# A fused attention and MLP kernel: a constant table moved to a hardware DMA queue, the last output tile in two column parts, and the planner's due dates moved by seeded steps

## The chip, the cores and the metric

The kernel runs on one core of one Trainium2 chip. The metric is the device time of one execution in microseconds (us), taken as the median of several runs. Runs of one kernel agree within about 0.3%. A comparison is called "faster" or "slower" only beyond 2%, but the 95% intervals of five rounds are about 0.2 to 0.4% wide to each side, so effects of 1 us in 320 us can be seen, though only just.

Engines are abbreviated as in the profile: PE is TensorE (matmuls), PEld its weight loads, DVE is VectorE, ACT is ScalarE, POOL is GpSimd and SP is SyncE. A "q" behind a name (SPq, ACTq) is the sequencer that issues DMAs. DMAs issued by SP and ACT go through hardware queues; those issued by POOL go through a software queue (in the first 14 us of the kernel before the profile lists 704 and 288 packets on two hardware queues and 1146 on one software queue).

## The reference

Four batches of eight heads of block-sparse attention (768 tokens, head size 64, blocks of 32; neighbours, first and last block, and three sampled blocks per block row), followed by an MLP-mixer layer:

```python
scores = scale * q @ k.T                       # masked to -1e9 outside the block pattern
attn   = softmax(scores);  x = attn @ v        # [4, 768, 512] after the heads are joined
a1  = alpha1 * x + beta1
tok = einsum('ts,bsd->btd', w_tok, a1)         # 768 x 768 over tokens
u   = x + lam * tok
a2  = alpha2 * u + beta2
out = u + lam * (relu(a2 @ w_ch1) @ w_ch2)     # 512 -> 2048 -> 512
```

## The kernel before

Heads are worked in 16 pairs. A pair has nine score units of 128 keys x 1024 queries; each unit is one exp on ACT (144 in all, numbered from 0 here). For the first six pairs the mask is a bias that is part of the score matmul: 24 more rows under the 64 rows of q and k. The rows under k are block indicators (`ind`), those under q are made at the start from a constant table (`tab`) and the sampled block numbers (`sampi`). This is the start of the kernel, where all else waits:

```python
    nc.gpsimd.dma_start(tab[MB, :], tab_dr.ap())                        # 4.5 KB, POOL's queue
    nc.sync.dma_start(sampi[MB, :], sampled_blocks.bitcast(I32))
    nc.scalar.dma_start(k2f[:, 0, :], pair_ap(k, 0, 0)[:, 0, :])        # 192 KB: k, first head
    nc.sync.dma_start(q2f[:, 0, :], pair_ap(q, 0, 0)[:, 0, :])
    nc.scalar.dma_start(identb[:], ident_dr.ap())                       # 32 KB: for PE transposes
    nc.sync.dma_start(kx2[0][MB, 0, :], ind_dr.ap())                    # indicator rows
    nc.sync.dma_start(q2f[:, 1, :], pair_ap(q, 0, 0)[:, 1, :])          # second head
    nc.sync.dma_start(k2f[:, 1, :], pair_ap(k, 0, 0)[:, 1, :])
    ...                                                                 # three more indicator copies
    nc.gpsimd.dma_start(ld["v"][0][:], pair_ap(v, 0, 0))
    keep_warm(8, 512)                  # eight matmuls of 512 columns on zeros
    ...                                # DVE: eqt, three maxima, mbb: the bias from tab and sampi
    ...                                # PE: two bias matmuls, mbb x indicator rows
    for w, cp in enumerate((nc.vector.tensor_copy, nc.scalar.copy)):
        t = transposes(gbT[w][:], lambda o: relp[:, 0, w, ts(o, P)], range(3))   # q, then k, head 0
        ...
    keep_warm(5, P)
    for j in range(1, 4):              # bias rows for the second head, and for the other buffer
        nc.sync.dma_start(qx2[j // 2][MB, j % 2, :], qx2[0][MB, 0, :])
```

Everything after this is put in order when the kernel is built. Each operation has an engine, an assumed duration, the operations that it depends on and a due date (a number on a scale of exps). A list scheduler goes through time and gives each free engine, of the operations that are ready, the one with the earliest due date. The order that comes out is fixed in the program; on the chip each engine takes its instructions strictly in that order.

```python
    op = pl.pe(("qk", i), occ, i - 0.7, e_qk, deps=..., ...)          # scores of unit i
    ex = pl.act(("exp", j), act(UN), j, ...)                          # exp of unit j
    pv = pl.pes(("pv", j, a), ..., j + 1.5, ...)                      # attn @ v
    tk = pl.pes(("tok", pi, g, j), NT, pe(1, P), FINE if pi < 4 else NT,
                dd + 1 + g, ...)                                      # token matmuls of pair pi
```

The channel MLP (`ch1`, `ch2`) ends the kernel; the last output tile is 16 matmuls of 512 columns, one add on DVE and one store of 256 KB.

The softmax here doesn't subtract the row's maximum and nothing guards it: scores larger than these inputs give would overflow.

## Time and profile before

| | before |
|---|---|
| time | 319.65 us, median of 4 (319.15 to 320.06) |
| span of the profiled run | 318.3 us |
| PE, DVE, ACT busy | 96%, 72%, 57% |
| first score matmul / exp 0 / exp 10 start | 8.22 / 9.27 / 20.58 us |
| last add to the end | 314.54 to 318.27: 3.73 us |

The chain of work that ended last, by engine, from the page of the kernel before:

```profile
PE 87%; ACT 6%; issue 3%; DVE 1%; DMA 1%; ACTq 0%; POOLq 0%
```

PE is the bottleneck, so only time that PE loses can be won. Busy time does not show this loss well, because the ends of matmuls are modelled. I took the start-to-start time of neighbouring matmuls instead, with the median of each form as its cost (32 ns for 65 columns, 56 for 128, 162 for 384, 216 for 512), and filled in records that are missing from the trace. What is left over is called PE loss below. It is 4.4 us up to 8.2 us (of which 1.4 us are the warm-up matmuls at half speed), 2.9 us from 8.2 to 14.4, 0.3 from there to 20, 3.3 us from 20 to 60, and then about 1 us in each 20 us until 240, which comes from a change of form: a score matmul on 64 rows costs about 95 ns more when it follows another form and when another follows it. After 260 us there is none. So the places to look at are the first 60 us and the tail.

The start, from the timelines of DVE and PE of the kernel before (start us, duration us, engine, line, operation, output<-input, shapes, count, idle time before it and what ended it):

```profile
5.39 0.22 DVE L358 TENSOR_TENSOR eqt<-sampi,tab 24x72 f32<-24x72 int32 x1 [4.16 <-DMA tab<-tab_c]
6.28 0.17 DVE L367 TENSOR_SCALAR mbb<-tab 24x24 bf16<-24x24 f32 x1
6.50 0.33 PE L388 MATMUL sps<-qk,mbb 24*24 24x384 bf16 x1 [1.96 <-DVE mbb L367]
6.92 0.51 PE L383 MATMUL gb<-identb,relp 128*128 128x128 bf16 x6
8.22 1.01 PE L821 MATMUL sps<-qk 88*128 88x512 bf16 x3 [0.51 <-DVE qk L402]
```

DVE stands 4.16 us for the table, then makes the bias; PE stands 1.96 us for the bias, transposes q and k with the identity matrix and starts the first scores at 8.22 us.

Busy time by stretch, from the windows of the kernel before (start:end, length, then busy us and count of each engine, the granted clock of PE, the time of the DMA packets as a share of the 16 DMA engines' time, which can come out over 1, GB/s):

```profile
core 0: us, PE busy (x) PEld busy (x) DVE busy (x) ACT busy (x) POOL busy (x), PEclk, DMA share, GB/s
8.20:14.40 6.20, 6.18 (x41) 4.03 (x41) 2.39 (x6) 4.28 (x5) 5.08 (x9) 0.50 1.08 155
20.00:60.00 40.00, 38.41 (x641) 31.44 (x639) 34.08 (x73) 35.93 (x41) 19.31 (x29) 1.00 1.20 214
```

In the first stretch PE runs at half speed: 41 matmuls fill 6.2 us. The clock record has the half speed from 7.57 to 14.40 us, that is 6.83 us or two times 3.41. The Trainium skill, "TensorE: Matmul & The Clock Gate", section "Part 1: The HAM clock gate", describes a free-running activity window of 3413 ns after which the clock is set; this trace agrees with that length. The second line is the stretch in which exps on ACT and the work of PE take turns: ACT is busy 35.93 of 40 us.

In that stretch, ACT's waits of the kernel before, from 20 to 62 us (engine line <- who ended the wait: us in total, times, longest):

```profile
ACT eT L850 <- PE sps L821: 3.9, 4, 1.9
```

And one place of it, from the timeline of PE of the kernel before:

```profile
30.63 0.59 PE L821 MATMUL sps<-qk 88*128 88x512 bf16 x3
31.45 2.17 PE L1088 MATMUL gb<-a1p,wtokT 128*128 128x128 bf16 x36 [0.23 <-ACT qk L428]
33.46 1.03 PE L821 MATMUL sps<-qk 88*128 88x512 bf16 x5
```

Token matmuls come as one block of 36. While it runs, PE makes no scores for ACT; in other places PE has only scores and waits for ACT to free their banks.

The tail of the kernel before, from the timeline at 314 to 318 us:

```profile
314.54 0.69 DVE L1295 TENSOR_TENSOR ot<-x_sb,gb 128x512 f32<-128x512 f32 x1 [2.77 <-PE gb L1273]
315.25 0.33 SPq L1314 DMA_DIRECT2D out_dram<-ot  x1
```

### The profile page before, as it was taken

Reading aid. Unit: us, or ns where it says so; the run is one execution under the profiler, and the core shown is the slowest. Engines: PE = TensorE matmul, PEld = TensorE weight load, DVE = VectorE, ACT = ScalarE, POOL = GpSimd, SP = SyncE. Lnnn points to the kernel's source line nnn. Section 1 sums busy time; section 2 is a strip of 40 time slices with the busy share of each in tenths; the row PEclk is TensorE's granted clock in tenths of the full one; section 3 lists DMA queues with packets and bytes.
Section 4 is the critical chain, followed back from the end, with each engine's and each line's share of the span. In section 5 each row is a group of like instructions: output and inputs, shape, how many; then the busy total and the mean of one; then the engine's idle time right before and its main releaser. Section 6 shows DMA issues by size and latency. Waiting matters only on the chain.

```text
span 318.3 us, 7655 instructions
## 1 busy us (share of the span) xinstructions
PE 306.7 (96%) x3204; PEld 188.5 (59%) x3237; DVE 230.5 (72%) x431; ACT 180.9 (57%) x217; POOL 55.9 (18%) x88
## 2 busy tenths in 40 slices
PE   5999999999999999999999999999999999999995
PEld 2677877756565665465656565655656565555542
DVE  3468979965879887697878696978778776555531
ACT  3799998788877557667685666666575400000000
POOL 3747354212404040213010100101000000000000
PEclk9599999999999999999999999999999999999999
DMA  6999999998737366276441411232102001100011
GB/s 147 152 243 208 209 203 205 202 134 138 116 59 140 69 115 129 60 136 127 58 113 55 101 59 53 69 96 61 27 33 60 33 2 47 55 33 33 35 66 66
DMA packets 46594, 31.40 MB, mean 99 GB/s; under 512 B 27192, under 2 KB 42016, under 8 KB 46560
## 3 DMA queue, kind: packets, MB, share of 16 engines
q0 software_dynamic: 16976, 17.44, 33.7%
q1 hardware_dynamic: 29296, 13.24, 15.8%
q8 instruction: 25, 0.41, 0.5%
q10 hardware_dynamic: 288, 0.23, 0.3%
q14 instruction: 9, 0.07, 0.1%
HBM read 30.86 MB, written 6.29 MB: 117 GB/s over the span
## 4 chain that ended last, share of the span: by engine, by line
PE 87%; ACT 6%; issue 3%; DVE 1%; DMA 1%; ACTq 0%; POOLq 0%
PE gb L1215 26%; PE gb L1273 25%; PE gb L876 11%; PE gb L1088 10%; PE sps L840 8%; ACT eT L850 5%; PE sps L821 5%; DMA tab<-tab_c 1%; PE gb L383 1%; PE sps L626 1%; ACT qk L428 1%; DVE x_sb L1112 0%; ACT uT L428 0%; DVE ub L1119 0%; PE gb L581 0%
## 5 line engine op out<-in xcount | busy, mean ns | idle before, releaser
L850 ACT ACTIVATE eT<-sps 128x1024 f16<-128x1024 f32 x144 | 140.5, 1025 | 37.6 <-PE sps L840 29.2
L1215 PE MATMUL gb<-uT,w1b 128*128 128x384 bf16 x512 | 100.8, 326 | 0.0
L1273 PE MATMUL gb<-w2b,hts 128*128 128x512 bf16 x351 | 91.4, 379 | 1.9 <-issue 0.3
L857 DVE TENSOR_TENSOR eT<-eT,msk 128x1024 f16<-128x1024 f16 x90 | 60.4, 684 | 10.1 <-ACT eT L850 10.1
L1245 DVE TENSOR_SCALAR hts<-gb,b1t 128x384 bf16<-128x384 f32 x75 | 46.2, 616 | 27.4 <-PE gb L1215 26.9
L1215 PEld LDWEIGHTS <-w1b 128*128 128x128 bf16 x512 | 46.4, 98 | 32.9 <-issue 1.2
L876 PEld LDWEIGHTS <-eT 128*128 128x128 f16 x1152 | 49.7, 98 | 24.7 <-issue 5.9
L876 PE MATMUL gb<-vext,eT 128*128 128x65 f16 x1152 | 57.3, 194 | 0.0
L1273 PEld LDWEIGHTS <-hts 128*128 128x128 bf16 x384 | 35.0, 98 | 32.8 <-issue 1.2
L1237 ACT ACTIVATE hts<-gb,b1t 128x384 bf16<-128x384 f32 x53 | 30.8, 582 | 29.7 <-PE gb L1215 27.8
L1088 PE MATMUL gb<-a1p,wtokT 128*128 128x128 bf16 x576 | 36.7, 219 | 0.2 <-ACT qk L428 0.2
L821 PE MATMUL sps<-qk 88*128 88x512 bf16 (+1 forms) x144 | 33.8, 342 | 2.0 <-ACT eT L850 1.2
L1088 PEld LDWEIGHTS <-wtokT 128*128 128x128 bf16 x576 | 33.5, 98 | 3.9 <-issue 1.5
L777 POOL DMA_DIRECT2D qk<-qk x20 | 12.2, 616 | 127.3 <-DMA qk<-q 71.3
L840 PE MATMUL sps<-qk 64*128 64x512 bf16 (+1 forms) x240 | 27.3, 326 | 0.1
L1295 DVE TENSOR_TENSOR ot<-x_sb,gb 128x512 f32<-128x512 f32 x24 | 16.5, 686 | 11.2 <-PE gb L1273 10.6
L1112 DVE TENSOR_TENSOR x_sb<-x_sb,gb 128x384 f32<-128x384 f32 x32 | 17.6, 551 | 9.5 <-PE gb L1088 9.4
L895 DVE TENSOR_TENSOR x_sb<-gb,rcp 128x384 f32<-128x384 f32 x32 | 17.8, 557 | 1.1
L1119 DVE TENSOR_TENSOR ub<-x_sb,a_bc 128x384 bf16<-128x384 f32 x32 | 17.7, 553 | 0.6
L821 PEld LDWEIGHTS <-qk 88*128 88x128 bf16 x144 | 13.0, 101 | 7.5 <-issue 2.7
L840 PEld LDWEIGHTS <-qk 64*128 64x128 bf16 x240 | 8.0, 94 | 15.0 <-issue 12.1
L1053 DVE TENSOR_TENSOR a1p<-a1p,b_bc 128x768 bf16<-128x768 bf16 (+1 forms) x20 | 15.8, 792 | 0.3
(66 smaller groups left out, 150.3 us busy)
## 6 DMA issues: line engine op xcount, KB each, us to landing
out_dram<-ot SPq DMA_DIRECT2D x24, 256.0 KB, 2.0
v<-in_v_dram POOLq DMA_DIRECT2D x16, 192.0 KB, 7.1
q<-in_q_dram POOLq DMA_DIRECT2D x15, 192.0 KB, 7.6
k<-in_k_dram POOLq DMA_DIRECT2D x15, 192.0 KB, 6.8
w1b<-in_moe_w_ch_dram POOLq DMA_DIRECT2D x4, 512.0 KB, 10.6
w2b<-in_moe_w_ch_dram POOLq DMA_DIRECT2D x4, 512.0 KB, 12.5
qk<-qk POOLq DMA_DIRECT2D x20, 96.0 KB, 2.2
wtk<-in_moe_w_tok_dram POOLq DMA_DIRECT2D x3, 384.0 KB, 9.6
```

The lines of the kernel that those rows point to most:

```text
L821: nc.tensor.matmul(spsT[sl(key)][:, o : o + w], kx2[i][0:KC, a, ts(jt, P)], qx2[i][0:KC, a, c : c + w], start=True, stop=True,)
L840: nc.tensor.matmul(spsT[sl(key)][:, o : o + w], kd[i][rows, h, g, :], qx2[i][rows, h, c : c + w], start=True, stop=True,)
L850: nc.scalar.activation(eTt[sl(("eT", i))][:], spsT[sl(key)][:], AF.Exp, bias=EXPB, scale=SCALE)
L857: nc.vector.tensor_tensor(out=e, in0=e, in1=msk[:, :, x : x + 512], op=ALU.mult)
L876: nc.tensor.matmul(bk[:, t * VW : t * VW + D + 1], eTt[sl(("eT", i))][:, ts(col, P)], vx[:, a, jt, 0 : D + 1], start=(r == 0), stop=(r >= ...
L895: nc.vector.tensor_tensor(out=x_sb[:, s0 : s0 + NT, h * D : (h + 1) * D], in0=o[:, :, 0:D], in1=rc[:].unsqueeze(2).broadcast_to([P, NT, D] ...
L1088: nc.tensor.matmul(tp[:, j, :], wtokT[:, s, ts(m * g + j, P)], a1p[sl(ak)][:, s, :], start=(s == 0), stop=(s == NT - 1),)
L1119: nc.vector.tensor_tensor(out=ub[sl(uk)][:, m * g : m * g + m, :], in0=x_sb[:, s0 + m * g : s0 + m * g + m, cs], in1=bc(a2_bc, m), op=ALU. ...
L1215: nc.tensor.matmul(bank(bk)[:, 0:HS], w1b[:, dk, ts(f, P)], uT[b % 3][:, dk, ts(hf, HS)], start=(dk == 0), stop=(dk == 3),)
L1237: nc.scalar.activation(htsT[hk][:, f, :], bank(bk)[:, 0:HS], AF.Relu, bias=b1t[:, f : f + 1], scale=1.0,)
L1245: nc.vector.tensor_scalar(out=htsT[hk][:, f, :], in0=bank(bk)[:, 0:HS], scalar1=b1t[:, f : f + 1], scalar2=0.0, op0=ALU.add, op1=ALU.max,)
L1273: nc.tensor.matmul(bank(ck)[:, 0:DM], htsT[hk][:, nk, ts(mt, P)], w2h["t"][:, nk, :], start=(nk == 0), stop=(nk == 15),)
```

## The change

Its intent: let the bias be ready sooner, shorten the tail, and find a better order. The 21 seeds each move the due dates of a random part of the operations by a random amount; where they come from is not told, but the numbers look like the kept steps of a long random search. The planner's loop is also rewritten to run faster at build time. Shortened:

```diff
+SEEDS = [4000001, 4000004, 4000014, ...]                  # 21 numbers
@@ Op
-        self.due = due
+        self.due = self.due0 = due
@@ Plan.run: candidates and their ready times are kept, not searched for anew (cut)
-                if best:
-                    op, (e, occ, vis) = min(best.values(), key=lambda x: x[0].due)
+                if best:
+                    op, (e, occ, vis) = min(best.values(), key=lambda x: (x[0].due, x[0].n))
@@ start
-    nc.gpsimd.dma_start(tab[MB, :], tab_dr.ap())
     nc.sync.dma_start(sampi[MB, :], sampled_blocks.bitcast(I32))
+    nc.scalar.dma_start(tab[MB, :], tab_dr.ap())
     nc.scalar.dma_start(k2f[:, 0, :], pair_ap(k, 0, 0)[:, 0, :])
-    keep_warm(8, 512)
+    keep_warm(7, 512)
@@ ch2, the output tiles (the slice cs is then used in matmuls, add and store)
-            for mt in range(3):
+            cuts = [(mt, 0, DM) for mt in range(3)]
+            if kk == 2 * B - 1:
+                cuts[2:] = [(2, 0, HS), (2, HS, DM)]         # HS = 384, DM = 512
+            for mt, c0, c1 in cuts:
@@ before pl.run()
+    for seed in SEEDS:
+        r = random.Random(seed)
+        part, step = r.choice([0.01, 0.03, 0.1, 0.3]), r.choice([0.5, 1.5, 4])
+        for op, due in zip(pl.ops, [op.due for op in pl.ops]):
+            if r.random() < part and op.due0 < 80:
+                op.due = due + r.gauss(0, step)
```

The built programs, compared engine by engine, show that table and warm-up alone change nothing else in the order; that the split with the new loop changes, apart from buffer numbers, fewer than a hundred of some 6500 rows on PE (matmuls and weight loads); and that the seeds reorder PE from about its row 85 to about its row 3390, thus in the first half.

More of the change, by code (lines that the diff above doesn't have):

```diff
@@ L1 @@
+import random
 from contextlib import ExitStack
@@ L44 @@
 FINE = 3
+SEEDS = [4000001, 4000004, 4000014, 4000025, 4000032, 4000033, 4000038, 4000259, 4000302, 4000315, 4000516, 4000717, 4000744, 4000751, 4000754, 4000772, 4000823, 4000910, 4001214, 4001220, 4002279]
 ORD = ((0, 2, 4, 1, 3, 5), (1, 3, 5, 0, 2, 4))
@@ L159, in run @@
         t = min(self.free.values())
-        todo = list(self.ops)
+        heirs = {}
+        for n, op in enumerate(self.ops):
+            op.n = n
+            before = {id(d): d for d in op.deps + op.after if d.start is None}
+            op.left = len(before)
+            for d in before:
+                heirs.setdefault(d, []).append(op)
+        cand = [op for op in self.ops if not op.left]
+        for op in cand:
+            op.ready = max([d.vis for d in op.deps] + [0])
+        count = len(self.ops)
         release = []
-        order = []
-        while todo:
+        while count:
             for r in [r for r in release if r[0] <= t]:
@@ L170, in run @@
                 best = {}
-                for op in todo:
-                    if any(d.vis is None or d.vis > t for d in op.deps):
+                idle = [e for e in self.free if self.free[e] <= t]
+                for op in cand:
+                    if op.ready > t:
                         continue
-                    if any(d.start is None for d in op.after):
+                    opts = [o for o in op.opts if o[0] in idle]
+                    r = self.reader.get(op.reads)
+                    if r and r[1] > t:
+                        opts = [o for o in opts if o[0] == r[0]]
+                    opts = [
+                        o
+                        for o in opts
+                        if o[0] not in best
+                        or (op.due, op.n) < (best[o[0]][0].due, best[o[0]][0].n)
+                    ]
+                    if not opts:
                         continue
                     taken = {}
-                    ok = True
                     for need in op.need:
@@ L180, in run @@
                         if p is None:
-                            ok = False
                             break
                         taken[p] = taken.get(p, 0) + 1
-                    if not ok:
-                        continue
-                    r = self.reader.get(op.reads)
-                    for o in op.opts:
-                        e = o[0]
-                        if r and r[0] != e and r[1] > t:
-                            continue
-                        if self.free[e] <= t and (e not in best or op.due < best[e][0].due):
-                            best[e] = (op, o)
-                for op in todo:
-                    if not op.urgent or any(d.vis is None for d in op.deps):
-                        continue
-                    for o in op.opts:
-                        if o[0] in best and best[o[0]][0].due > op.due:
-                            wait = max([d.vis for d in op.deps]) - t
-                            if 0 < wait < best[o[0]][1][1]:
-                                del best[o[0]]
+                    else:
+                        for o in opts:
+                            best[o[0]] = (op, o)
+                if not best:
+                    break
+                for op in cand:
+                    if op.urgent and op.ready > t:
+                        for o in op.opts:
+                            if o[0] in best and best[o[0]][0].due > op.due:
+                                if op.ready - t < best[o[0]][1][1]:
+                                    del best[o[0]]
                 if best:
-                    op, (e, occ, vis) = min(best.values(), key=lambda x: x[0].due)
+                    op, (e, occ, vis) = min(best.values(), key=lambda x: (x[0].due, x[0].n))
                     for need in op.need:
@@ L220, in run @@
                         self.exps += 1
-                    todo.remove(op)
+                    cand.remove(op)
+                    count -= 1
+                    for h in heirs.get(id(op), []):
+                        h.left -= 1
+                        if not h.left:
+                            h.ready = max([d.vis for d in h.deps] + [0])
+                            cand.append(h)
                     op.emit(op)
@@ L225, in run @@
             later += [r[0] for r in release if r[0] > t]
-            later += [d.vis for op in todo for d in op.deps if d.vis is not None and d.vis > t]
-            if todo and not later:
-                raise RuntimeError(f"stuck: {[o.name for o in todo[:20]]}")
-            if todo:
+            later += [op.ready for op in cand if op.ready > t]
+            if count and not later:
+                raise RuntimeError(f"stuck: {[o.name for o in cand[:20]]}")
+            if count:
                 t = min(later)
-        return t
 @with_exitstack
@@ L1265, with e_c2 @@
             pc = []
-            for mt in range(3):
+            cuts = [(mt, 0, DM) for mt in range(3)]
+            if kk == 2 * B - 1:
+                cuts[2:] = [(2, 0, HS), (2, HS, DM)]
+            for mt, c0, c1 in cuts:
                 t = 3 * hf + mt
-                ck = ("cp", kk, mt)
+                cs = slice(c0, c1)
+                ck = ("cp", kk, mt, c0)
                 for r in range(4):
-                    def e_c2(op, hk=hk, ck=ck, mt=mt, r=r):
+                    def e_c2(op, hk=hk, ck=ck, mt=mt, r=r, cs=cs):
                         for nk in range(4 * r, 4 * r + 4):
                             nc.tensor.matmul(
-                                bank(ck)[:, 0:DM],
+                                bank(ck)[:, cs],
                                 htsT[hk][:, nk, ts(mt, P)],
-                                w2h["t"][:, nk, :],
+                                w2h["t"][:, nk, cs],
                                 start=(nk == 0),
@@ L1282 @@
                         ("ch2", kk, mt, r),
-                        pe(4, 2048),
-                        d0 + 18 + (4 * mt + r) * 18 / 12,
+                        pe(4, 4 * (c1 - c0)),
+                        d0 + 18 + (4 * mt + r) * 18 / 12 + c0 / 100,
                         e_c2,
@@ L1291, with e_ot @@
                     pc.append(c2)
-                okey = ("ot", kk, mt)
-                def e_ot(op, okey=okey, ck=ck, b=b, t=t):
+                okey = ("ot", kk, mt, c0)
+                def e_ot(op, okey=okey, ck=ck, b=b, t=t, cs=cs):
                     nc.vector.tensor_tensor(
-                        out=ot[sl(okey)][:],
-                        in0=x_sb[:, b % NXB * NT + t, :],
-                        in1=bank(ck)[:, 0:DM],
+                        out=ot[sl(okey)][:, cs],
+                        in0=x_sb[:, b % NXB * NT + t, cs],
+                        in1=bank(ck)[:, cs],
                         op=ALU.add,
@@ L1303 @@
                     ("ot", kk, mt),
-                    dve(512),
+                    dve(c1 - c0),
                     d0 + 18 + 18 / 12 * 4 * mt - 2,
@@ L1311, with e_out @@
                 OT[(b, t)] = o
-                def e_out(op, okey=okey, b=b, t=t):
+                def e_out(op, okey=okey, b=b, t=t, cs=cs):
                     nc.sync.dma_start(
-                        out[b].rearrange("(p o) d -> p o d", o=NT)[:, t, :], ot[sl(okey)][:]
+                        out[b].rearrange("(p o) d -> p o d", o=NT)[:, t, cs],
+                        ot[sl(okey)][:, cs],
                     )
```

## The prediction

> **What bounds it now.** TensorE (PE): 87% of the chain of waits that ended last. From start-to-start times of the matmuls (median of each form as its cost: 32 ns for 65 columns, 56 for 128, 162 for 384, 216 for 512; absent records filled in) I find hardly a recoverable gap from 60 us on: about 1 us in each 20 us, nearly all of it 95 ns at each entry to and exit from the 64-row score matmuls. What can be won lies before 60 us and after the last matmul:
>
> - Start: `tab` is issued on the GpSimd queue at 1.24 us and lands at 5.37; VectorE waits 4.2 us for it (waits view). The mask bias is ready at 6.45, the bias matmuls start at 6.50 after 2.1 us of idle PE, the first score matmul at 8.22.
> - Clock: half speed from 7.57 to 14.40 us, two windows of 3.41 us; PE loses about 2.9 us. The Trainium skill, "TensorE: Matmul & The Clock Gate", section "Part 1: The HAM clock gate", describes such a window and a throttle after low activity; this trace agrees.
> - 14.4 to 60 us: about 3.6 us of PE loss, mostly before score matmuls that wait for exp on ACT (1.02 us each).
> - Tail: last VectorE add 0.69 us, output DMA 1.98 us, closing 1.0 us: 4.1 us after the last matmul starts.
>
> **What the change does.**
>
> 1. `tab` on the ACT queue. Its neighbours on hardware queues land in 2.0 to 2.5 us. The Trainium skill, "DMA: Bandwidth & Descriptors", section "SWDGE vs HWDGE vs iDMA", also has hardware descriptor generation as the faster setup. So `tab` lands near 2.5 to 2.8 us and the bias is ready near 4.0 (the small VectorE operations took 1.06 us). Seven warm-up matmuls end at 4.18. The bias matmuls start at 4.2 to 4.4 unless the indicator rows (landed only at 5.55 before, behind contention) hold them. The first score matmul is at about 6.1 (5.8 to 7.3): gain 2.0 us.
> 2. With the PE gap nearly closed, the clock may stay full; I give it 60%. It then saves about 2 of the 2.9 us, as ACT becomes the limit. Estimate: 1.2 us.
> 3. Due dates. The order on PE, DVE and ACT changes in the first half: token matmuls and transposes that ran as one block near 31 us are cut up and put between scores. I expect a third of the 3.6 us: 1.2 us; it can be nothing.
> 4. Last tile in 384 and 128 columns: 16 more matmuls, no more PE work (162+56 against 216 ns). The last add is about 0.3 us instead of 0.69, the last transfer 64 KB instead of 256: 0.7 us.
> 5. The rewritten planner loop is build time only: without the seeds the order is nearly the old one.
>
> All of it is on the critical path, as PE runs without gaps afterwards: 2.0 + 1.2 + 1.2 + 0.7 = 5.1 us.
>
> **Prediction: 314.6 us, 312.0 to 317.5.** Faster by over 2% (under 313.4): 0.24; within 2%: 0.74; slower: 0.02.
>
> **What would show it.** Step 1: VectorE idle under 2 us before its first compare, first score matmul near 6.1. Step 2: granted clock over 0.9 in 8 to 20 us (0.73 before). Step 3: less PE idle ended by exp in 14 to 60 us. Step 4: last add to end under 3.1 us (3.73 before).
>
> **What would make it wrong.** The indicator rows still land at 5.5 (1 us less); the clock falls anyway; the new order makes PE stand before operands not yet loaded; or the seeds recover most of the early loss (312).

## The result

| | before | after |
|---|---|---|
| time, median of 4 | 319.65 us (319.15 to 320.06) | 314.70 us (314.35 to 315.75) |
| ratio, 95% interval | | 0.9851 (0.9823 to 0.9880) |
| first score matmul / exp 0 / exp 10 start | 8.22 / 9.27 / 20.58 us | 7.34 / 8.08 / 18.73 us |
| PE loss 8.2 to 14.4 us / 20 to 60 us | 2.9 / 3.3 us | 1.7 / 0.6 us |
| last add to the end | 3.73 us | 2.78 us |

A ratio is the mean time of one kernel's runs over that of the other's of the same rounds, so it is not quite the ratio of the medians. In a later series the same two kernels gave 0.9867 (0.9846 to 0.9887). The change saves 1.3 to 1.5%; by the 2% rule it counts as the same.

The chain that ended last, by engine, from the page of the changed kernel:

```profile
PE 93%; DVE 3%; DMA 1%; issue 1%; ACT 1%; ACTq 0%
```

ACT's share went from 6 to 1%: PE waits for exps hardly at all now. The start, from the timelines of DVE and PE of the changed kernel (line numbers are 19 to 23 higher than before):

```profile
2.50 0.23 DVE L377 TENSOR_TENSOR eqt<-sampi,tab 24x72 f32<-24x72 int32 x1 [1.27 <-DMA sampi<-in_sampled_blocks_dram]
3.39 0.17 DVE L386 TENSOR_SCALAR mbb<-tab 24x24 bf16<-24x24 f32 x1
4.64 0.35 PE L407 MATMUL sps<-qk,mbb 24*24 24x384 bf16 x1 [0.28 <-DMA qk<-ind_c]
6.20 0.49 PE L402 MATMUL gb<-identb,relp 128*128 128x128 bf16 x6 [1.05 <-DMA identb<-ident_c]
7.34 1.33 PE L840 MATMUL sps<-qk 88*128 88x512 bf16 x5 [0.37 <-DVE qk L421]
```

The table no longer holds anything. The bias is ready at 3.56 instead of 6.45 us, 2.9 us sooner, and the bias matmuls start 1.9 us sooner. But a new wait stands behind them: PE waits 1.05 us for the identity matrix, which landed at 4.04 us before and lands at 6.16 us now. The first score matmul is only 0.9 us sooner.

The windows of the changed kernel, the columns as above:

```profile
8.20:14.40 6.20, 6.10 (x67) 4.32 (x65) 3.26 (x8) 5.39 (x6) 3.31 (x6) 0.73 1.13 202
20.00:60.00 40.00, 39.76 (x671) 32.76 (x670) 35.37 (x75) 38.10 (x43) 17.66 (x26) 1.00 1.21 212
```

The clock was at half speed for one window of 3.41 us (8.15 to 11.56 us) instead of two. From 20 to 60 us PE ran 671 matmuls instead of 641, and ACT was busy 38.10 us instead of 35.93. ACT's waits in 20 to 62 us, and the place with the token matmuls in the timeline of PE, both of the changed kernel:

```profile
ACT eT L869 <- PE sps L840: 1.2, 2, 0.8
```

```profile
29.99 1.16 PE L1107 MATMUL gb<-a1p,wtokT 128*128 128x128 bf16 x18
...
31.24 0.60 PE L840 MATMUL sps<-qk 88*128 88x256 bf16 x3
31.67 1.17 PE L1107 MATMUL gb<-a1p,wtokT 128*128 128x128 bf16 x18
32.68 0.60 PE L840 MATMUL sps<-qk 88*128 88x512 bf16 x3
33.12 1.17 PE L1107 MATMUL gb<-a1p,wtokT 128*128 128x128 bf16 x18
```

The block of 36 is cut into parts of 18 with scores between them. The tail, from the timeline of the changed kernel:

```profile
309.03 0.56 DVE L1318 TENSOR_TENSOR ot<-x_sb,gb 128x384 f32<-128x384 f32 x1 [1.91 <-PE gb L1296]
309.61 0.96 SPq L1337 DMA_DIRECT2D out_dram<-ot  x2
309.92 0.29 DVE L1318 TENSOR_TENSOR ot<-x_sb,gb 128x128 f32<-128x128 f32 x1 [0.34 <-PE gb L1296]
```

The last add took 0.29 us instead of 0.69, and from its start to the end it is 2.78 us instead of 3.73.

### The profile page after: what moved, and what is told of

Its sections match the earlier page's. It is cut to its first block, busy times and chain, and to the rows that moved or that the text cites. A ratio compares the mean times of both kernels' runs of the same rounds, so it can differ in the third digit from the quotient of the medians.

```text
span 312.7 us, 7687 instructions
## 1 busy us (share of the span) xinstructions
PE 304.4 (97%) x3221; PEld 188.3 (60%) x3252; DVE 231.4 (74%) x434; ACT 179.7 (57%) x215; POOL 55.7 (18%) x87
## 4 chain that ended last, share of the span: by engine, by line
PE 93%; DVE 3%; DMA 1%; issue 1%; ACT 1%; ACTq 0%
PE gb L1234 27%; PE gb L1296 26%; PE gb L895 12%; PE gb L1107 10%; PE sps L859 8%; PE sps L840 7%; PE gb L402 2%; DMA identb<-ident_c 1%; PE sps L645 1%; DVE qk L449 1%; ACT eT L869 1%; PE gb L600 0%; DVE x_sb L1131 0%; DVE ub L1138 0%; DVE a1p L1072 0%
## 5 line engine op out<-in xcount | busy, mean ns | idle before, releaser
L1296 PE MATMUL gb<-w2b,hts 128*128 128x512 bf16 (+2 forms) x369 | 91.3, 369 | 1.8 <-issue 0.2
L895 PE MATMUL gb<-vext,eT 128*128 128x65 f16 x1152 | 58.0, 194 | 0.1
L1296 PEld LDWEIGHTS <-hts 128*128 128x128 bf16 x400 | 35.7, 97 | 31.2 <-issue 0.7
L1256 ACT ACTIVATE hts<-gb,b1t 128x384 bf16<-128x384 f32 x52 | 30.1, 582 | 28.1 <-PE gb L1234 26.4
L1107 PE MATMUL gb<-a1p,wtokT 128*128 128x128 bf16 x576 | 38.2, 219 | 0.1
L840 PE MATMUL sps<-qk 88*128 88x512 bf16 (+1 forms) x144 | 33.0, 333 | 0.7 <-DVE qk L421 0.4
L1318 DVE TENSOR_TENSOR ot<-x_sb,gb 128x512 f32<-128x512 f32 (+2 forms) x25 | 16.6, 664 | 10.1 <-PE gb L1296 9.6
L1061 DVE TENSOR_TENSOR a1p<-x_sb,a_bc 128x768 bf16<-128x768 f32 (+1 forms) x20 | 15.8, 791 | 0.2
```

The source lines that it names most:

```text
L840: nc.tensor.matmul(spsT[sl(key)][:, o : o + w], kx2[i][0:KC, a, ts(jt, P)], qx2[i][0:KC, a, c : c + w], start=True, stop=True,)
L895: nc.tensor.matmul(bk[:, t * VW : t * VW + D + 1], eTt[sl(("eT", i))][:, ts(col, P)], vx[:, a, jt, 0 : D + 1], start=(r == 0), stop=(r >= ...
L1107: nc.tensor.matmul(tp[:, j, :], wtokT[:, s, ts(m * g + j, P)], a1p[sl(ak)][:, s, :], start=(s == 0), stop=(s == NT - 1),)
L1256: nc.scalar.activation(htsT[hk][:, f, :], bank(bk)[:, 0:HS], AF.Relu, bias=b1t[:, f : f + 1], scale=1.0,)
L1296: nc.tensor.matmul(bank(ck)[:, cs], htsT[hk][:, nk, ts(mt, P)], w2h["t"][:, nk, cs], start=(nk == 0), stop=(nk == 15),)
```

## The experiments

Each run was compared with the kernel before on the same chip in five rounds. All gave correct results. There were four series, not all on the same chip, so ratios are compared, not medians.

### One part at a time

`tab_only` is the kernel before with two edits:

```diff
-    nc.gpsimd.dma_start(tab[MB, :], tab_dr.ap())
+    nc.scalar.dma_start(tab[MB, :], tab_dr.ap())      # behind sampi's issue on sync
-    keep_warm(8, 512)
+    keep_warm(7, 512)
```

> The old kernel with the table on the ACT queue and seven warm-up matmuls; no other change. Theory A (the gain is a sum of independent parts, read from the two traces): the first score matmul comes 0.9 us sooner (near 7.3 instead of 8.2), a throttled window less gives up to 1.2 us; 317.6 to 318.8 us against 319.7. Rival B (what is won at the start is lost again to the exp pace on ACT, so that only the new order brings anything): within 0.3 us of the old kernel. Both expect the identity matrix to land late (near 6 us) and PE to wait for it about 1 us.

`tail_only` is the changed kernel without the seeds, with table and warm-ups as before:

```diff
-    for seed in SEEDS: ...
-    nc.scalar.dma_start(tab[MB, :], tab_dr.ap())
+    nc.gpsimd.dma_start(tab[MB, :], tab_dr.ap())
-    keep_warm(7, 512)
+    keep_warm(8, 512)
```

> The old kernel with the new planner loop and the last tile in parts of 384 and 128 columns; table on GpSimd, eight warm-ups, no seeds. Theory A: last add to end 2.8 us instead of 3.7, so 318.7 us (0.95 less). Rival B: the planner's new loop or the other bank numbers cost something, or the second output transfer queues behind the first, and the gain is under 0.4 us.

`seeds_only` is the changed kernel with the old table, warm-ups and tail:

```diff
-            if kk == 2 * B - 1:
-                cuts[2:] = [(2, 0, HS), (2, HS, DM)]
-    nc.scalar.dma_start(tab[MB, :], tab_dr.ap())
+    nc.gpsimd.dma_start(tab[MB, :], tab_dr.ap())
-    keep_warm(7, 512)
+    keep_warm(8, 512)
```

> The changed kernel with table on GpSimd, eight warm-ups and the last tile whole again: the seeds alone. Theory A (parts add up): PE loss in 20 to 60 us falls from 3.3 to about 0.6 us, 317.0 us (2.7 less). Rival B (the seeded order needs the early start, because it was planned for it): loss in 20 to 60 us stays over 2 us, and the time is over 318.3 us.

`no_seeds` is the changed kernel without the loop over the seeds:

```diff
-    for seed in SEEDS: ...
```

> The changed kernel without the loop over the seeds: table, warm-ups and tail changed, order as planned before. Theory A: 317.4 us (2.7 slower than the changed kernel), PE loss in 20 to 60 us about 3.3 us. Rival B (the early start lets the old order do as well): 315.5 us or less.

Measured:

| kernel | median us | ratio to before (95%) | first score | exp 10 starts | exp 10 to end | PE loss 20 to 60 us |
|---|---|---|---|---|---|---|
| before | 319.8 | 1 | 8.22 | 20.58 | 297.70 | 3.3 |
| tab_only | 318.52 | 0.9968 (0.9949 to 0.9987) | 7.96 | 19.78 | 297.56 | 3.2 |
| tail_only | 318.60 | 0.9967 (0.9944 to 0.9991) | 8.14 | 18.75 | 296.92 | 3.3 |
| seeds_only | 316.68 | 0.9908 (0.9888 to 0.9928) | 8.62 | 20.34 | 294.87 | 0.65 |
| no_seeds | 318.38 | 0.9972 (0.9947 to 0.9997) | 8.25 | 19.57 | 296.77 | 3.3 |
| after (as first measured) | 314.70 | 0.9851 (0.9823 to 0.9880) | 7.34 | 18.73 | 293.97 | 0.59 |

The column "exp 10 to end" is the useful find. It splits a run into a start, which differs from execution to execution, and a rest that repeats to a tenth of a microsecond for kernels of the same order. From it:

- The seeds are worth 297.70 - 294.87 = 2.83 us without, and 296.77 - 293.97 = 2.80 us with the early start and the new tail. So theory A of `seeds_only` holds, and the rival, that the seeded order needs the early start, falls; so does the rival of `no_seeds`, that the early start lets the old order do as well (its PE loss stayed at 3.3 us). The timings agree: 0.9908 is 2.9 us of 319.8.
- The tail is worth 297.70 - 296.92 = 0.78 us, and 294.87 - 293.97 = 0.90 us with the seeds. Between the two kernels without seeds that have the table on ACT's queue (`tab_only` to `no_seeds`) it is 0.79 us. The rival of `tail_only`, a gain under 0.4 us, falls.
- Table and warm-ups act before exp 10 alone, and there they are hard to see. With the table on POOL's queue exp 10 started at 20.58, 18.75 and 20.34 us in the three profiles, with it on ACT's queue at 19.78, 19.57 and 18.73 (and, in later runs, 19.91 and 19.92). The timings say 1.0 us (0.4 to 1.6) for `tab_only`, but `no_seeds` has the tail's 0.8 us too and gains only 0.9 us in all, which leaves about nothing for the table. Between 0 and 1 us is what can be said; neither theory of `tab_only` is excluded.

Both expected a late identity matrix in `tab_only`, and so it was, in the waits of PE of that run:

```profile
PE gb L383 <- DMA identb<-ident_c: 1.3, 1, 1.3
```

The windows of 20 to 60 us of `seeds_only` and of `no_seeds`, in this order, show where the seeds work:

```profile
20.00:60.00 40.00, 39.77 (x673) 32.92 (x671) 35.49 (x75) 38.36 (x43) 19.30 (x28) 1.00 1.19 212
```

```profile
20.00:60.00 40.00, 38.20 (x634) 31.21 (x632) 34.18 (x72) 35.86 (x41) 18.75 (x27) 1.00 1.22 211
```

### What holds the start

The second series had the changed kernel again as its measure.

> The changed kernel once more, as the measure for the next three on the same chip: 314.7 us, 0.985 of the old kernel.

It gave 315.66 us, 0.9867 (0.9846 to 0.9887). Its profiled execution had a worse start than the first one: the identity matrix landed at 7.12 us, the first score matmul came at 8.53 us and exp 10 at 19.91 us, and the rest was 293.97 us again. So one and the same kernel differs by 1.2 us in its start.

`ident_first` issues the identity matrix ahead of k:

```diff
     nc.scalar.dma_start(tab[MB, :], tab_dr.ap())
+    nc.scalar.dma_start(identb[:], ident_dr.ap())
     nc.scalar.dma_start(k2f[:, 0, :], pair_ap(k, 0, 0)[:, 0, :])
-    nc.scalar.dma_start(identb[:], ident_dr.ap())
```

> The changed kernel with the identity matrix issued on the ACT queue before the 192 KB of k, instead of after it. Theory A (PE waits 1.05 us for the identity matrix at 5.1 to 6.2 us, and all later work shifts with it): it lands before 5 us, the first score matmul is near 6.3 instead of 7.3, and the time falls by 0.8 to 1.0 us to 313.8. Rival B (the early part is paced by the exps and by the loads, and slack behind eats an earlier start): the first score matmul is earlier, but the time falls by less than 0.3 us.

Measured: 315.70 us, 0.9874 (0.9857 to 0.9891), no gain against the 0.9867 of the changed kernel. The identity matrix landed at 4.05 us as hoped, but k, now behind it, landed at 5.56 us instead of 4.2 to 4.4, as ACT's waits of this run show:

```profile
ACT relp L397 <- DMA k2f<-in_k_dram: 2.1, 1, 2.1
```

The first score matmul came at 7.22 us, a little earlier than in either run of the changed kernel, and not at 6.3. Rival B is what was seen: an earlier start, no earlier end. Exp 10 started at 19.50 us.

`v_late` tries the other explanation for the late identity matrix, that v's transfer starts 0.65 us sooner since POOL no longer issues the table. An unused second load of the table puts v back to 1.9 us:

```diff
+    tab2 = pp.tile([P, 2 * NBLK], FP, name="tab2", tag="tab2")
+    nc.gpsimd.dma_start(tab2[MB, :], tab_dr.ap())
     nc.gpsimd.dma_start(ld["v"][0][:], pair_ap(v, 0, 0))
```

> The changed kernel with a second, unused load of the table on the GpSimd queue ahead of v, so that v is issued at about 1.9 us, as in the old kernel, instead of 1.26. Theory A1 (the identity matrix is late because v's packets start sooner and share the DMA engines): it lands near 4.6 us, PE's wait for it goes to 0, the first score matmul is about 1 us earlier. Rival A2 (it is late because it is issued 0.72 us later, behind k): it still lands after 5.7 us.

Measured: 314.25 us, 0.9830 (0.9810 to 0.9850). In the profiled execution the identity matrix landed at 4.89 us and the first score matmul came at 6.47 us, as A1 expects. Taken alone this would have looked like a proof. The same kernel was run again in the third series:

> The kernel of v_late once more, as the measure for the next one on the same chip: 314.2 us, 0.983 of the old kernel.

It gave 315.06 us, 0.9859 (0.9823 to 0.9895), and the wait was back, in PE's waits of `v_late_again`:

```profile
PE gb L404 <- DMA identb<-ident_c: 1.6, 1, 1.6
```

The identity matrix landed at 7.00 us. So A1 falls: with v late, the landing was 4.89, 7.00 and, in `told_loads` below, 7.16 us. What separates the traces is the issue of the matrix itself. Issued second on ACT's queue (at 1.17 or 1.35 us) it landed at 3.99 to 4.16 us in all five traces of such kernels; issued third (at 1.89), it landed at 6.05 to 7.16 us in eight of nine. That is the first half of A2, "issued 0.72 us later". Its second half, "behind k", is not the reason: in the kernel before, the matrix also stood behind the same 192 KB of k and landed at 4.04 us. Whether the later time or the larger number of loads issued before it counts was not separated. The Trainium skill, "DMA: Bandwidth & Descriptors", section "Issuing engines are not separate DMA queues", says that DMAs "will ultimately run on the same 16 DMA engines and interleave with each other, regardless of the engine that started them". These traces agree: in the changed kernel the DMA share is 0.97 from 1.9 to 6.2 us, while the matrix is on its way, and bringing one load forward delayed another.

### What the clock is worth

`fill_gap` puts 16 matmuls on zeros into PE's gap before the transposes, where they delay nothing:

```diff
     # after the two bias matmuls
+    keep_warm(16, P)
     first_cast(0, 0, nc.vector.tensor_copy)
```

> The changed kernel with 16 warm-up matmuls of 128 columns put into PE's gap between the bias matmuls and the first transposes; they end before the identity matrix lands. Theory A (the throttle follows PE's activity in a 3.4 us window, and the throttled window costs PE time that is not won back): the clock stays full after 5 us in most executions and the time falls by 0.5 to 1.2 us. Rival B (while ACT's exps set the pace, PE's clock does not matter): the clock stays full and the time is the same within 0.3 us.

Measured: 314.56 us, 0.9837 (0.9819 to 0.9854), against 0.9867 for the changed kernel of the same series: about 1.0 us less. The intervals overlap a little, and the filler was run in one series only, so the gain is likely rather than sure. In the profiled execution exp 10 started at 18.30 us, the earliest of all runs, although the first score matmul was late (7.89 us). The speed of PE is read from the matmuls, here the first five of the scores, 2048 columns, of `ident_first` and of `fill_gap`, in the timelines:

```profile
7.22 1.89 PE L840 MATMUL sps<-qk 88*128 88x512 bf16 x5
```

```profile
7.89 1.14 PE L841 MATMUL sps<-qk 88*128 88x512 bf16 x5 [0.37 <-DVE qk L422]
```

In `fill_gap` matmuls ran at full speed from 4.54 us; in `after_again` none did before 12.38. So the times speak for theory A, that the clock is worth something, and against rival B, without proving it.

These profiles do not show that the filler made the difference. The two bias matmuls at about 4.6 us of 384 columns (0.16 us at full speed) start 0.16 us apart in `fill_gap` and 0.27 us apart in `after_again`: the clock differed before the first filler matmul (4.95 us). They start 0.16 to 0.19 us apart in four of the 14 profiled executions (`before`, `after`, `v_late`, `fill_gap`) and 0.27 to 0.29 us in the other ten, where PE then ran at half speed until 10.5 to 15.9 us, or until 5.85 us in `ident_fill` below, which has filler. So in most executions the clock was not lost in the gap: the warm-up matmuls had not raised it in the first place. Of the three executions without filler where it was up, it stayed up in one, `v_late`, where the matrix landed early (4.89 us).

The profile's own clock column does not show this; in the windows of `after_again` it reads 1.00 in the very stretch in which 28 matmuls fill 4 us:

```profile
8.40:12.40 4.00, 3.97 (x28) 2.47 (x28) 2.08 (x6) 2.94 (x5) 2.38 (x4) 1.00 1.15 200
```

### What paces exps 4 to 10

`told_loads` starts from `v_late`, and gives the planner landing times near those that were measured, so that early scores are not placed behind transposes of data that come late:

```diff
-    deps=[landed(("f", i), 5500 + 500 * i)],          # second head's q and k
+    deps=[landed(("f", i), 6300 + 1100 * i)],
-    LD[("v", 0)] = landed(("v", 0), 6000)
+    LD[("v", 0)] = landed(("v", 0), 8000)
```

> The kernel of v_late, with the planner told landing times near those of its trace (second-head q 6.3 and k 7.4 us instead of 5.5 and 6.0; v 8.0 instead of 6.0), so that the scores of the third exp stand before the second head's transposes and not behind them. Theory A (in v_late the early start is lost because PE stands, in its order, before transposes of operands that have not landed: exp number 10 comes at 18.7 us although the first came at 7.1): exps run back to back from 7.1, exp number 10 comes near 17.3 us, and the time is 0.8 to 1.4 us under v_late. Rival B (loads of later pairs, or exp on ACT, pace the stretch up to 60 us in any case): exp number 10 comes sooner, exp number 30 within 0.3 us of v_late's 40.3 us, and so does the end.

Measured: 317.42 us, 0.9935 (0.9904 to 0.9966), 2.4 us slower than `v_late_again`. Theory A falls in this form, and rival B, which also expected an earlier exp 10, is not what was seen. The rest after exp 10 is the same (294.09 us), so all of the harm is before it: exp 10 started at 22.20 us. The identity matrix was late in this execution (7.16 us, first scores at 8.57), so the new order was of no use, and PE ran at half speed until 15.92 us, 3.7 us longer than in `v_late_again`. At half speed PE fell behind ACT, as ACT's waits from 6 to 20 us show:

```profile
ACT eT L871 <- PE sps L842: 2.8, 4, 1.1
```

The last run, `ident_fill`, joins `ident_first` with filler in the place where its PE stood:

```diff
     nc.scalar.dma_start(tab[MB, :], tab_dr.ap())
+    nc.scalar.dma_start(identb[:], ident_dr.ap())
     nc.scalar.dma_start(k2f[:, 0, :], pair_ap(k, 0, 0)[:, 0, :])
-    nc.scalar.dma_start(identb[:], ident_dr.ap())
...
     for w, cp in enumerate((nc.vector.tensor_copy, nc.scalar.copy)):
+        if w == 1:
+            keep_warm(16, P)
         t = transposes(...)
```

> The changed kernel with the identity matrix issued before k (as in ident_first) and 16 warm-up matmuls of 128 columns between the first head's transposes of q and of k, where ident_first's PE stands idle. In ten traces of kernels with the seeded order the time from exp number 10 to the end is 294.0 us (294.9 with the whole last tile), so the kernel's time is told by when exp number 10 starts. Theory A (an earlier start and a full clock both count): first score matmul near 7.2, clock full, exp number 10 near 17.7 us, 313.6 us, 0.980 to 0.982 of the old kernel. Rival B (with the clock full the start does not count, because loads pace the first ten exps): exp number 10 at 18.2 us or later, 0.983 to 0.985 as fill_gap.

(Where this says ten traces: there were seven of kernels with the seeds and the new tail at that time, and one with the seeds and the old tail.)

Measured: 315.46 us, 0.9877 (0.9846 to 0.9908). The clock was full from 5.85 us, the first score matmul came at 7.36 and the first four exps ran without a gap from 8.18 us, and yet exp 10 came at 19.73 us. Theory A falls. Rival B was right that a load sets the pace, but did not name it, and its ratio (0.983 to 0.985) was not met. The timeline of PE in that run shows it:

```profile
11.20 0.38 PE L842 MATMUL sps<-qk 88*128 88x512 bf16 x1
13.46 0.38 PE L842 MATMUL sps<-qk 88*128 88x512 bf16 x1 [1.88 <-DMA qk<-qk]
```

The load named is the copy of the bias rows to the second head (the first of three copies of 36 KB in the last lines of the start, above). Exp 4 is the first that needs it, because unit 4 is half of the first head and half of the second. With this known, the other traces fall into line:

| execution | copy issued | landed | matmul that needs it | exp 4 | exp 10 |
|---|---|---|---|---|---|
| fill_gap | 5.55 | 11.89 | 12.03 | 12.44 | 18.30 |
| v_late | 5.77 | 12.27 | 12.41 | 12.82 | 18.69 |
| after | 5.68 | 12.33 | 12.46 | 12.87 | 18.73 |
| ident_first | 6.62 | 13.09 | 13.23 | 13.64 | 19.50 |
| ident_fill | 6.50 | 13.32 | 13.46 | 13.87 | 19.73 |
| v_late_again | 5.96 | 12.49 | 13.39 | 13.84 | 19.66 |
| after_again | 5.92 | 12.36 | 13.63 | 14.07 | 19.91 |
| before | 7.52 | 11.80 | 14.18 | 14.70 | 20.58 |

In the first five the matmul starts 0.13 to 0.14 us after the landing, exp 4 follows 0.41 us later, exp 10 5.8 to 5.9 us after that, and the end 294.0 us after exp 10. Those five executions fit a limit set by the landing of one 36 KB copy, which takes 6.3 to 6.8 us from its issue. In the last three the copy had long landed; there PE at half speed, after a late first score, was behind it. In the six profiled executions not listed (the four parts, `told_loads` and `tok_later8`) the copy also landed 0.45 to 3.1 us before the matmul. So, in these traces, an earlier first score than about 8 us buys nothing (exp 0 at 7.12 us in `v_late`, exp 10 later than in `fill_gap`), and a full clock buys only the time down to the landing. The waits of PE in the changed kernel do not name the copy, because PE filled the time with other work until just before the landing. Its chain in order of time does have the place, in this step of 0.10 us between the previous work and the matmul, followed by the exp:

```profile
12.36 0.10 issue
12.46 0.39 PE sps L840
...
12.87 2.05 ACT eT L869 x2
```

That the copy is the limit is argued from the match in five traces and from PE's named wait of 1.88 us in `ident_fill`; it is not shown by an experiment that moves the copy alone.

### What the seeds do

`tok_later8` is `no_seeds` with one rule by hand:

```diff
-                    dd + 1 + g,
+                    dd + 1 + g + (8 if pi < 3 else 0),     # due date of the token matmuls
```

> The kernel of no_seeds with one hand-made rule instead of seeds: the due dates of the token matmuls of the first three pairs are 8 units later, so that they are cut up and fill PE between scores, where before 36 stood in one block. Theory A (the seeds win because PE's filler is spread so that neither PE nor ACT waits for the other before 60 us): PE loss in 20 to 60 us falls from 3.3 to 1.3 us or less, and the time to 316.4 us (2 us less than no_seeds). Rival B (the seeds' gain is made of many small moves, and spreading these matmuls alone does little): loss stays over 2.3 us and the time over 317.6 us.

Measured: 316.62 us, 0.9904 (0.9873 to 0.9935). The rest after exp 10 is 295.01 us, against 296.77 for `no_seeds` and 293.97 with the seeds: 1.76 of the 2.80 us, or 63%. PE loss in 20 to 60 us is 1.7 us, between the 1.3 of theory A and the 2.3 of the rival. The window line of this run:

```profile
20.00:60.00 40.00, 39.46 (x662) 32.28 (x659) 33.60 (x74) 37.33 (x41) 17.15 (x25) 1.00 1.21 210
```

In its trace the block of 36 near 31 us has become one of 18 and three of 9, with scores between them. So nearly two thirds of what the seeds gain can be had by one rule that can be told: the token matmuls of the first pairs had due dates so early that they ran in a block as soon as they could, and later dates make them filler. The rest lies in moves that I did not take apart.

## Why the prediction came out as it did

The total was predicted at 314.6 us (312.0 to 317.5) and measured at 314.7 us, with "within 2%" as the likeliest. The sum was right by luck: the terms for start and clock were too large by over 2 us together, the term for the seeds was too small by 1.6 us, and the errors nearly cancelled.

1. *Table, start: 2.0 us predicted, with step 2 3.2 us; together about 0.6 to 1.1 us measured* (0.9851 and 0.9867 of 319.8 are 4.8 and 4.3 us, less 2.8 for the seeds and 0.8 to 0.9 for the tail). The table itself did as told: it landed at 2.20 us, 1.5 us after its issue, DVE's first compare waited 1.27 us, and the bias was ready at 3.56 us. The step that failed is "the first score matmul is at about 6.1". It leaves out the identity matrix, which landed at 4.04 us before; the change makes it the third issue on ACT's queue instead of the second, and it came at 6.16 and 7.12 us. The prediction looked at the indicator rows as the risk, and those were no trouble (they landed at 4.60 us). It also took an early first score to be won for good, and the copy of the bias rows, landing near 12.3 us, seems to take that back.
2. *Clock: 60% for a full clock, 1.2 us expected.* In the two profiled executions of the changed kernel it was not full: one slow window in the first, half speed until 12.4 us in the second. For the first the mechanism fits: the clock was up at 4.64 us and fell at 8.15, after the gap that the change leaves open, since the new wait for the identity matrix is where the old one for the table was. In the second the clock could not stay full, because the warm-up had not raised it; the prediction did not reckon with that. What a full clock is worth, about 1.0 us by `fill_gap`, is likely but not sure.
3. *Seeds: 1.2 us predicted, 2.8 us measured.* The place and the mechanism were right (ACT's waits in 20 to 62 us fell from 3.9 to 1.2 us, PE's own waits for exps in the whole run from 1.2 to 0.2, and cutting the token block by hand gives 63% of the gain). The size was off: I took a third of the 3.6 us of PE loss in 14 to 60 us to be recoverable, and four fifths of the loss in 20 to 60 us went (3.27 to 0.59).
4. *Tail: 0.7 us predicted, 0.8 to 0.9 measured.* The add took 0.29 us as told, and the rest came from the smaller store.
5. *The planner's loop: no effect predicted, none seen.* `no_seeds` and `tail_only` have the new loop and 3.3 us of PE loss in 20 to 60 us, as before.

That all of it is on the critical path, because PE runs without gaps afterwards, was right for everything after exp 10: 294.0 us (293.95 to 294.09) in eight executions of six kernels, whatever the start. It was not right for the start itself, where a later wait can swallow the gain.

The two lowest ratios are those of `v_late` (0.9830, and 0.9859 when it was run again) and of `fill_gap` (0.9837, run once), against 0.9867 for the changed kernel in the second series, where both first ran. Which of the two is the faster these runs do not tell.

## What to carry to other kernels

When a late load is brought forward, follow every load that shares its queue or the DMA engines up to the first use, because at a start where the engines are full the wait moves to the next in line: here from the table to the identity matrix, and from there, as far as five traces show, to a 36 KB copy that nobody waited for before. A point in the program from which the rest repeats to a tenth of a microsecond separates small effects much better than total times do, and it shows that one profiled execution of the start proves little: `v_late` looked like a proof until it was run again. In a fixed order by due dates, work that is not urgent should carry late dates, so that it fills gaps, and not early ones, so that it comes in a block.

## What the Trainium skill lacked or had wrong

- "DMA: Bandwidth & Descriptors", section "Anatomy of one DMA — SWDGE (gpsimd) path", fits about 2.0 us plus size for one DMA. While the DMA engines are busy at the start (share 0.97 from 1.9 to 6.2 us in the changed kernel), small transfers took far longer: 4.1 us for the 4.5 KB table on the GpSimd queue, 4.2 to 5.3 us for the 32 KB identity matrix issued third on ACT's queue in eight of nine executions, and 5.9 to 6.8 us for the 36 KB copy on SP's queue in the eight executions with the seeds and the table on ACT's queue. No page that I read tells what a small transfer takes behind full queues.
- "TensorE: Matmul & The Clock Gate", section "Part 1: The HAM clock gate", gives slow after an idle and fast after a busy window, and not how busy is enough. In the kernel before the clock fell after a window (4.16 to 7.57 us) with 1.45 us of PE busy, so not an idle one, and was not raised after one (7.57 to 10.98 us) with 2.90 of 3.41 us busy. Where there was a slow stretch in the runs without filler, it ended anywhere from 10.5 to 15.9 us.
- The same page, section "Seeing it yourself", warns that clock events in traces are unreliable, and these runs agree: in `after_again` and `v_late_again` the record was empty and the mean clock read 1.00, while matmuls of 512 columns started 427 ns apart until about 12.3 us. The page could add that a missing record reads as full speed, and that the distance between matmuls is what to trust.
- "TensorEngine Tiling (Array Packing)", section "Key Properties", says that a change of tiling mode drains TensorE, and gives no cost for it there. Here a change between score matmuls on 64 rows and the other forms costs about 95 ns on entry and 92 ns on exit, which is nearly all the loss of PE after 60 us.
